# First product worked on in PSUM, softmax's small sums in one PSUM bank, every other weight chunk's low part on VectorE

## The chip, the cores and the metric

The kernel runs on one core of a Trainium2 chip. The metric is the device time of one execution in microseconds (us). Engines are named as the profile names them: PE is TensorE (matmuls, with PEld for its weight loads), DVE is VectorE, ACT is ScalarE, POOL is GpSimd, SP is SyncE, which issues the DMAs. All of them but SP work through instruction queues of their own, strictly in order.

## The reference, cut to what matters

Three stages follow each other: an attention with two kinds of masks, a two-layer MLP with a PReLU whose slope is given per hidden unit, and a routed mixture of eight experts.

```python
# attention: B, H, S, D = 4, 8, 576, 64
scores = scale * np.matmul(q, k.transpose(0, 1, 3, 2))
scores = np.where(masks[None, :, :, :], scores, -1000000000.0)   # local (heads 0-3) or strided (heads 4-7), both causal
scores = scores - np.max(scores, axis=-1, keepdims=True)
attn = np.exp(scores)
attn = attn / (np.sum(attn, axis=-1, keepdims=True) + 1e-09)
x = np.matmul(attn, v)                     # -> 2304 tokens x 512
# MLP, d_ff = 2048
h = x @ w_in
g = np.maximum(h, 0.0) + alpha * np.minimum(h, 0.0)
x = g @ w_out
# experts: the best of 8 by x @ w_gate, relu(x @ w1[e]) @ w2[e], weighted by the gate
```

## The kernel before, in words

**Attention.** The work is cut into groups (a pair of heads of one batch and some of its rows, four score blocks of up to 128 x 128 each, some groups two of 72 x 72). A step s of the attention lets each engine work on another group: ACT makes the exponentials of group s-1 (`att_exp`, L280, one ACTIVATE per block, each of which also sums its row into a column of `sm`), PE makes the scores of group s (`att_scores`, L228 and L234), PE and ACT make the values of group s-3 (`att_values`, `att_store`), PE transposes group s-2 (`att_transpose`, L312, copied out by ACT in L314), DVE takes the row maxima of group s (`att_max`: two reductions L252 and a scaling L255 of the small tile `nm`), and DVE and POOL normalize group s-1 (`att_norm`: L294 and L295 on the small tile `sm`, then L296 on POOL). Scores of a step lie in PSUM: in the first thirteen steps those of even steps in the first half of `sl_bank` and in bank X, those of odd steps in two banks "h"; in later steps always in `sl_bank` and X.

**Weights of the MLP.** They come in 16 chunks of float64 words. A chunk is decoded by ACT (`decode_a`, L401), DVE (`decode_b`, L405 and L406, and `decode_s`, L412) and then split into a high part by ACT (L420) and a low part by POOL (L421, 1024 columns of 128 partitions). The chunks 0 to 4 are decoded beside the first attention, the others one per iteration of the first block of the MLP.

**MLP.** Six blocks of 384 tokens, 16 chunks each; one chunk of one block is an iteration n. `mlp_in` makes the first product in one of the two banks "h" (12 matmuls, L438 to L440), `mlp_act` is the PReLU (ACT: L447 into the SBUF tile `a`, L448 into `bn`; DVE: L449 on both), `mlp_split` gives the high part `gh` (ACT, L458) and the low part `gl` (L460, on POOL in the first block, on DVE later), and `mlp_out` makes the second product (9 matmuls, L473 to L475). Iteration n issues the first product and the PReLU of n+2 and the second product of n, and in between up to one step of the attention.

**What sets the order.** The program's order is written by hand (`tc.manual_schedule()`), queue by queue. In the first block of the MLP, DVE's queue in iteration n reads: L294 and L295 of group s-1, L371 (the low part of the values of group s-3), L449 of n+2, the maxima of group s, then L405, L406 and L412 of chunk n+5. POOL's reads: L296, L421 of chunk n+4, L460 of n+2. The waits between the engines are put in by the program from what instructions write and read; in PSUM they go by whole banks.

Of the kernel before, what the change touches and what calls it, by code (L numbers as in the profile page):

```python
# [15 lines left out]
P = 128  # L16
# [11 lines left out]
BLK = 384  # L28
# [21 lines left out]
# Splits ahead of the turn of the tokens of the place after next, by the kinds of three places in a row.  # L50
# [3 lines left out]
# When the parts of the second plan, its lists and its indices come: (place, position).  # L54
WHEN = ((0, 7), (1, 1), (1, 1), (1, 4), (1, 6))
OHP = 12
# Groups that VectorE normalizes, and groups whose scores come after matmuls that keep TensorE awake.
NRV = (9,)
FS = {2: 2}
# Parts of the first two products of the MLP that run between the last steps of the first attention.  # L60
# [23 lines left out]
def attention_prelu_mlp_routed_experts_kernel(  # L84
# [40 lines left out]
    with tc.manual_schedule():  # L125
# [20 lines left out]
        # A visit is a pair of heads of a batch and the groups of its rows that are worked on in turn.  # L146
# [94 lines left out]

        def att_max(gi):
# [7 lines left out]
            if b < PE_MASK:  # L250
                for h2 in range(2):
                    nc.vector.tensor_reduce(  # L252
                        out=nm[:r, h2 * nj : (h2 + 1) * nj], in_=sc[h2][:r, 0:nj, :kk], axis=X, op=ALU.max, negate=True
                    )
                nc.vector.tensor_scalar_mul(nm[:r, :nu], nm[:r, :nu], SCALE)  # L255
# [15 lines left out]
        def att_exp(gi):  # L271
# [5 lines left out]
            sm = apool.tile([P, 4], F32, tag="sm", name="sm", bufs=3)  # L277
# [12 lines left out]
        def att_norm(gi):  # L290
            local, js, r, kk = shape_of(gi)
            nu = 2 * len(js)
            pt, sm = p_t[gi]
            nc.vector.tensor_scalar_add(sm[:r, :nu], sm[:r, :nu], 1e-9)  # L294
            nc.vector.reciprocal(sm[:r, :nu], sm[:r, :nu])  # L295
            (nc.vector if gi in NRV else nc.gpsimd).tensor_tensor(  # L296
                out=pt[:r, :nu, :kk],
                in0=pt[:r, :nu, :kk],
                in1=sm[:r, :nu].unsqueeze(2).to_broadcast([r, nu, kk]),
                op=ALU.mult,  # L300
            )
# [90 lines left out]
        # A weight comes as a float64, two words; it leaves as the sum of two float32r.  # L392
# [24 lines left out]
        def decode_c(c):  # L417
# [3 lines left out]
            nc.gpsimd.tensor_tensor(out=w[:, 1024:], in0=t, in1=w[:, :1024].bitcast(F32), op=ALU.subtract)  # L421
# [20 lines left out]
        def mlp_act(n):  # L442
            c = n % NC1
            ph = h_t.pop(n)
            a = xpool.tile([P, BLK], F32, tag="a", name="a", bufs=2)
            bn = xpool.tile([P, BLK], F32, tag="bn", name="bn", bufs=1)
            nc.scalar.activation(out=a, in_=ph[:, :BLK], func=AF.Relu)  # L447
            nc.scalar.activation(out=bn, in_=ph[:, :BLK], func=AF.Relu, scale=-1.0)  # L448
            nc.vector.scalar_tensor_tensor(  # L449
                out=a, in0=bn, scalar=nalpha[:, c : c + 1], in1=a, op0=ALU.mult, op1=ALU.add  # L450
            )
            h_t[n] = a

        def mlp_split(n):
            a = h_t.pop(n)
            gh = xpool.tile([P, BLK], F32R, tag="gh", name="gh", bufs=3)
            gl = xpool.tile([P, BLK], F32R, tag="gl", name="gl", bufs=2)
            nc.scalar.activation(out=gh, in_=a, func=AF.Copy)  # L458
            eng = nc.gpsimd if n < NC1 else nc.vector
            eng.tensor_tensor(out=gl, in0=a, in1=gh.bitcast(F32), op=ALU.subtract)  # L460
# [97 lines left out]
        def route_parts(blk):  # L558
            """One-hot choice, weight and place in its expert's list of each token of a block."""
# [76 lines left out]
        def plan_parts(early):  # L636
            """A column is a list of up to 128 tokens of one expert, a place's tokens one or two columns. The
            first EARLY columns hold pairs of full lists of the tokens before the last block. The others
            of each expert come in pairs from C_P on, a last odd one from C_S on; but a last one of FEW
            tokens or less has its column from C_Q on."""  # L640
# [209 lines left out]
        # A place is work on one expert: "P" on two columns, "S" on one, "Q" on one of few tokens. "P" makes  # L850
        # the hidden values with the tokens in the free dimension. "Q" takes the weights as they are, its
        # tokens stand in each quarter of the partitions, and each quarter makes its part of a row.
# [14 lines left out]
        def load_expert(t, h, always=False):  # L867
            """The first (h = 0) or second weight of place t's expert, unless it is there already."""
# [230 lines left out]
        def att_step(s, tags, ttag, vtag):  # L1099
            """One step of the attention, each engine's part on what the others did a step ago."""  # L1100
# [21 lines left out]
        def decode(k, n):  # L1122
            """The first n steps of a weight's decoding, those that are still to be done."""
# [40 lines left out]
        def gathers(ahead, places=NPL):  # L1164
            """The next tokens, as far as there is room for them."""
# [113 lines left out]
        def split(t, h, some=range(4)):  # L1279
            """Splits, and loads what comes next in the place of what was split."""  # L1280
# [103 lines left out]
        def some(kind, n, end, step):  # L1384
            """The places of a kind from the n-th on, as far as they are used, step by step."""
# [106 lines left out]
```

## Time and profile before

| | |
|---|---|
| median of three runs | 833.76 us (832.44 to 834.35) |
| span of the profiled execution, from the first to the last instruction | 831.9 us |
| median less that span, taken for what lies around it | 1.9 us |
| PE busy over the span | 784.2 us (94%) |
| DVE busy | 478.4 us (58%) |
| ACT busy | 427.3 us (51%) |
| POOL busy | 244.5 us (29%) |

The page's shares are means over stages with different limits. In the strip of 40 slices PE is at 9 tenths or more from the eighth slice (about 150 us) on nearly to the end, and between 6 and 8 tenths in the slices before, where DVE stands at 8 and 9 and POOL at 5 to 7. The stretch up to 150 us holds the first attention and the decoding of all 16 weight chunks.

### The profile page before, as it was taken

The numbers are of one execution on the slowest core, as the hardware profiler recorded it, in microseconds if no ns is written. First come the engines' busy times: TensorE is split into PE (matmuls) and PEld (weight loads), VectorE is DVE, ScalarE is ACT, GpSimd is POOL, SyncE is SP. The second block draws the span as 40 slices with busy tenths as digits, with TensorE's granted clock in tenths as the row PEclk, the third lists the DMA queues.
The fourth block names the chain that finished last, engine by engine and source line by source line (L and its number), as shares of the span: only waits on it lengthen the run. The fifth ranks groups of instructions, "written<-read, shape, count | busy, mean of one in ns | idle before, by whom it ended". The sixth has DMA issues, their size and how long they took to land. (4 is left out here: it accounts for less than half of the span.)

```text
span 831.9 us, 13663 instructions
## 1 busy us (share of the span) xinstructions
PE 784.2 (94%) x5032; PEld 659.6 (79%) x5035; DVE 478.4 (58%) x988; ACT 427.3 (51%) x1033; POOL 244.5 (29%) x168
## 2 busy tenths in 40 slices
PE   7687878999999999999999999999989998999995
PEld 4475766788888888888799898889878876878884
DVE  5989999345534554556333424757595447854422
ACT  6756665454455444665433333356534656655542
POOL 2756655200000000110000000032483354546422
PEclk9998999999999999999999999999999999999998
DMA  9716511101200121011000100362224577777421
GB/s 342 298 43 244 190 33 45 44 22 56 84 18 1 47 86 64 1 45 39 1 1 1 39 0 1 149 244 103 77 77 147 194 258 255 285 288 267 161 90 38
DMA packets 22621, 91.04 MB, mean 109 GB/s; under 512 B 3082, under 2 KB 7312, under 8 KB 15376
## 3 DMA queue, kind: packets, MB, share of 16 engines
q1 hardware_dynamic: 18816, 78.52, 26.6%
q0 software_dynamic: 3728, 11.55, 3.9%
q8 instruction: 41, 0.67, 0.3%
q14 instruction: 36, 0.29, 0.1%
HBM read 105.78 MB, written 9.97 MB: 139 GB/s over the span
## 5 line engine op out<-in xcount | busy, mean ns | idle before, releaser
L449 DVE SCALAR_TENSOR_TENSOR a<-bn,nalpha,a 128x384 f32<-128x384 f32 x96 | 73.2, 763 | 116.4 <-ACT bn L448 116.0
L438 PE MATMUL h<-xh,w 128*128 128x384 f32 x384 | 130.4, 340 | 0.4 <-ACT bn L448 0.4
L440 PE MATMUL h<-xh,w 128*128 128x384 f32 x384 | 129.9, 338 | 0.0
L439 PE MATMUL h<-xl,w 128*128 128x384 f32 x384 | 129.7, 338 | 0.0
L296 POOL TENSOR_TENSOR p<-p,sm 96x512 f32<-96x512 f32 (+2 forms) x47 | 48.7, 1036 | 267.6 <-DVE sm L295 255.3
L473 PE MATMUL acc<-w,gh 128*128 128x512 f32 x288 | 126.9, 441 | 0.0
L888 DVE TENSOR_TENSOR wx<-raw,wx 128x1024 fp32r<-128x1024 f32 x72 | 97.1, 1392 | 46.6 <-ACT wx L886 46.3
L475 PE MATMUL acc<-w,gl 128*128 128x512 f32 x288 | 115.8, 402 | 0.3 <-POOL gl L460 0.3
L474 PE MATMUL acc<-w,gh 128*128 128x512 f32 x288 | 115.6, 401 | 0.0
L886 ACT ACTIVATE wx<-raw 128x1024 fp32r<-128x1024 f32 x96 | 94.6, 1056 | 7.3 <-DMA raw<-in_wexp_dram 7.3
L447 ACT ACTIVATE a<-h 128x384 f32<-128x384 f32 x96 | 47.1, 491 | 99.7 <-PE h L440 99.6
L1042 PE MATMUL acc<-wx,hh 128*128 128x512 f32 x304 | 96.8, 400 | 0.0
L888 POOL TENSOR_TENSOR wx<-raw,wx 128x1024 fp32r<-128x1024 f32 x24 | 63.1, 2629 | 89.1 <-ACT wx L886 88.9
L438 PEld LDWEIGHTS h<-xh,w 128*128 128x128 f32 x384 | 73.1, 190 | 5.1 <-ACT bn L448 0.8
L439 PEld LDWEIGHTS h<-xl,w 128*128 128x128 f32 x384 | 72.9, 190 | 4.0
L440 PEld LDWEIGHTS h<-xh,w 128*128 128x128 f32 x384 | 72.6, 189 | 0.0
L895 POOL DMA_INDIRECT xg<-rows,idx_in x23 | 29.4, 1278 | 145.7 <-DVE a L449 139.3
L458 ACT ACTIVATE gh<-a 128x384 fp32r<-128x384 f32 x96 | 49.9, 520 | 42.6 <-DVE a L449 42.5
L475 PEld LDWEIGHTS acc<-w,gl 128*128 128x128 f32 x288 | 55.5, 193 | 14.2 <-POOL gl L460 0.8
L1042 PEld LDWEIGHTS acc<-wx,hh 128*128 128x128 f32 x304 | 56.5, 191 | 11.1
L473 PEld LDWEIGHTS acc<-w,gh 128*128 128x128 f32 x288 | 55.2, 192 | 11.1 <-issue 0.8
L460 DVE TENSOR_TENSOR gl<-a,gh 128x384 fp32r<-128x384 f32 x80 | 44.5, 556 | 28.7 <-ACT gh L458 16.6
(260 smaller groups left out, 1573.7 us busy)
## 6 DMA issues: line engine op xcount, KB each, us to landing
raw<-in_wexp_dram SPq DMA_DIRECT2D x64, 1024.0 KB
raw<-in_wp_dram SPq DMA_DIRECT2D x16, 1024.0 KB
qk<-in_qkv_dram SPq DMA_DIRECT2D x10, 576.0 KB
rows<-stage SPq DMA_DIRECT2D x15, 256.5 KB
v<-in_qkv_dram SPq DMA_DIRECT2D x8, 320.0 KB
qk<-in_qkv_dram SPq DMA_DIRECT2D x4, 384.0 KB
v<-in_qkv_dram SPq DMA_DIRECT2D x6, 256.0 KB
qk<-in_qkv_dram SPq DMA_DIRECT2D x4, 224.0 KB
```

Of the source, the lines that this page charges most:

```text
L296: (nc.vector if gi in NRV else nc.gpsimd).tensor_tensor(out=pt[:r, :nu, :kk], in0=pt[:r, :nu, :kk], in1=sm[:r, :nu].unsqueeze(2).to_broadc ...
L438: mm(ph[:, :BLK], w_in(c, 0, k), xh[:, k, :], start=(k == 0), stop=False)
L439: mm(ph[:, :BLK], w_in(c, 0, k), xl[:, k, :], start=False, stop=False)
L440: mm(ph[:, :BLK], w_in(c, 1, k), xh[:, k, :], start=False, stop=(k == KD - 1))
L449: nc.vector.scalar_tensor_tensor(out=a, in0=bn, scalar=nalpha[:, c : c + 1], in1=a, op0=ALU.mult, op1=ALU.add)
L458: nc.scalar.activation(out=gh, in_=a, func=AF.Copy)
L473: mm(o, gh[:, t], w_out(c, 0), start=(c == 0), stop=False)
L474: mm(o, gh[:, t], w_out(c, 1), start=False, stop=False)
L475: mm(o, gl[:, t], w_out(c, 0), start=False, stop=(c == NC1 - 1))
L886: nc.scalar.activation(out=w[:, :1024], in_=raw, func=AF.Copy)
L888: eng.tensor_tensor(out=w[:, 1024:], in0=raw, in1=w[:, :1024].bitcast(F32), op=ALU.subtract)
L1042: mm(po[i], h[:, h0 : h0 + P], wk[:, w0 : w0 + 512], start=st, stop=sp)
```

## The change

Three things are done. First, the PReLU works in the PSUM bank of the first product: ACT writes the second Relu back into the bank, DVE writes its result there, and both halves of the split read it there; the tile `bn` goes. The subtraction for `gl` is DVE's in every block. Second, two small tiles of the softmax get a stage in PSUM, in the last 64 columns of `sl_bank`: the row maxima before their scaling, and the sums of the exponentials; the scaled maxima and the sums with 1e-9 added still go to SBUF. Third, the low part of every odd weight chunk is subtracted by DVE instead of POOL.

```diff
+        def few(gi, n):
+            c = 448 + 32 * n + 4 * (gi % 8)
+            return sl_bank[:, c : c + 4]
...
             if b < PE_MASK:
+                raw = few(gi, 0)
                 for h2 in range(2):
                     nc.vector.tensor_reduce(
-                        out=nm[:r, h2 * nj : (h2 + 1) * nj], in_=sc[h2][:r, 0:nj, :kk], axis=X, op=ALU.max, negate=True
+                        out=raw[:r, h2 * nj : (h2 + 1) * nj], in_=sc[h2][:r, 0:nj, :kk], axis=X, op=ALU.max, negate=True
                     )
-                nc.vector.tensor_scalar_mul(nm[:r, :nu], nm[:r, :nu], SCALE)
+                nc.vector.tensor_scalar_mul(nm[:r, :nu], raw[:r, :nu], SCALE)
...
-            sm = apool.tile([P, 4], F32, tag="sm", name="sm", bufs=3)
+            sm = few(gi, 1)
...
-            pt, sm = p_t[gi]
-            nc.vector.tensor_scalar_add(sm[:r, :nu], sm[:r, :nu], 1e-9)
+            pt, raw = p_t[gi]
+            sm = apool.tile([P, 4], F32, tag="sm", name="sm", bufs=3)
+            nc.vector.tensor_scalar_add(sm[:r, :nu], raw[:r, :nu], 1e-9)
...
-            nc.gpsimd.tensor_tensor(out=w[:, 1024:], in0=t, in1=w[:, :1024].bitcast(F32), op=ALU.subtract)
+            eng = nc.vector if c % 2 else nc.gpsimd
+            eng.tensor_tensor(out=w[:, 1024:], in0=t, in1=w[:, :1024].bitcast(F32), op=ALU.subtract)
...
+            v = ph[:, :BLK]
             a = xpool.tile([P, BLK], F32, tag="a", name="a", bufs=2)
-            bn = xpool.tile([P, BLK], F32, tag="bn", name="bn", bufs=1)
-            nc.scalar.activation(out=a, in_=ph[:, :BLK], func=AF.Relu)
-            nc.scalar.activation(out=bn, in_=ph[:, :BLK], func=AF.Relu, scale=-1.0)
+            nc.scalar.activation(out=a, in_=v, func=AF.Relu)
+            nc.scalar.activation(out=v, in_=v, func=AF.Relu, scale=-1.0)
             nc.vector.scalar_tensor_tensor(
-                out=a, in0=bn, scalar=nalpha[:, c : c + 1], in1=a, op0=ALU.mult, op1=ALU.add
+                out=v, in0=v, scalar=nalpha[:, c : c + 1], in1=a, op0=ALU.mult, op1=ALU.add
             )
-            h_t[n] = a
+            h_t[n] = v
...
-            nc.scalar.activation(out=gh, in_=a, func=AF.Copy)
-            eng = nc.gpsimd if n < NC1 else nc.vector
-            eng.tensor_tensor(out=gl, in0=a, in1=gh.bitcast(F32), op=ALU.subtract)
+            nc.scalar.activation(out=gh, in_=v, func=AF.Copy)
+            nc.vector.tensor_tensor(out=gl, in0=v, in1=gh.bitcast(F32), op=ALU.subtract)
```

Since PSUM is tracked by whole banks, the small sums bring waits with them. DVE's queue at the start of the attention (steps 0 and 1; in brackets whose count an instruction waits for) reads before:

```order
L252 TENSOR_REDUCE nm<-sl_bank 96x2 [waits PE_49]
L252 TENSOR_REDUCE nm<-X 96x2 [waits PE_49]
L255 TENSOR_SCALAR nm<-nm 96x4 [waits DVE_49]
L252 TENSOR_REDUCE nm<-h 96x2 [waits PE_49] x2
L255 TENSOR_SCALAR nm<-nm 96x4 [waits DVE_49]
L294 TENSOR_SCALAR sm<-sm 96x4 [waits Activation_49]
```

and now (lines stand seven further on in the changed kernel):

```order
L258 TENSOR_REDUCE sl_bank<-sl_bank 96x2 [waits PE_49]
L258 TENSOR_REDUCE sl_bank<-X 96x2 [waits DVE_49,PE_49]
L261 TENSOR_SCALAR nm<-sl_bank 96x4 [waits DVE_49]
L258 TENSOR_REDUCE sl_bank<-h 96x2 [waits DVE_49,PE_49,Activation_49]
L258 TENSOR_REDUCE sl_bank<-h 96x2 [waits DVE_49,PE_49]
L261 TENSOR_SCALAR nm<-sl_bank 96x4 [waits DVE_49]
L301 TENSOR_SCALAR sm<-sl_bank 96x4
```

The second reduction of a group now waits for the first, and the reductions of step 1 wait for ACT: for the last exponential of step 0, which writes its sum into the same bank.

ACT's exponentials of steps 0 and 1 stand like this before:

```order
L280 ACTIVATE p,sm<-sl_bank,nm 96x128 [waits DVE_49,PE_49]
L280 ACTIVATE p,sm<-sl_bank,nm 96x128
L280 ACTIVATE p,sm<-X,nm 96x128 [waits PE_49]
L280 ACTIVATE p,sm<-X,nm 96x128
L280 ACTIVATE p,sm<-h,nm 96x128 [waits DVE_49,PE_49]
```

and now:

```order
L286 ACTIVATE p,sl_bank<-sl_bank,nm 96x128 [waits DVE_49,PE_49]
L286 ACTIVATE p,sl_bank<-sl_bank,nm 96x128 [waits Activation_49]
L286 ACTIVATE p,sl_bank<-X,nm 96x128 [waits PE_49,Activation_49]
L286 ACTIVATE p,sl_bank<-X,nm 96x128 [waits Activation_49]
L286 ACTIVATE p,sl_bank<-h,nm 96x128 [waits DVE_49,PE_49,Activation_49]
```

Each exponential now waits for ACT's own one before it. The matmuls of an even step's scores, which write `sl_bank`, wait in the same way for the last exponential of the step before (their rows read alike in both programs; the count that they wait for is another).

In the first block of the MLP, one iteration of DVE's queue reads before, from the maxima of a group to the PReLU of the next iteration:

```order
L252 TENSOR_REDUCE nm<-sl_bank 126x2 [waits PE_49]
L252 TENSOR_REDUCE nm<-X 126x2 [waits PE_49]
L255 TENSOR_SCALAR nm<-nm 126x4 [waits DVE_49]
L405 TENSOR_SCALAR stage<-stage 128x1024
L406 SCALAR_TENSOR_TENSOR stage<-raw_581,stage 128x1024 [waits DMAHW3_49,DVE_49]
L412 SCALAR_TENSOR_TENSOR stage<-raw_581,stage 128x1024 [waits DVE_49]
L294 TENSOR_SCALAR sm<-sm 126x4 [waits Activation_49]
L295 RECIPROCAL sm<-sm 126x4 [waits DVE_49]
L371 TENSOR_TENSOR xl<-T,xh 128x192 [waits Activation_49]
L449 SCALAR_TENSOR_TENSOR a<-bn,nalpha,a 128x384 [waits Activation_49,Pool_49]
```

and now, from the same step of the program, with the PReLU ahead of it:

```order
L457 SCALAR_TENSOR_TENSOR h<-h,nalpha,a 128x384 [waits Activation_49]
L429 TENSOR_TENSOR w<-stage,w 128x1024 [waits Activation_49]
L258 TENSOR_REDUCE sl_bank<-sl_bank 126x2 [waits PE_49]
L258 TENSOR_REDUCE sl_bank<-X 126x2 [waits DVE_49,PE_49]
L261 TENSOR_SCALAR nm<-sl_bank 126x4 [waits DVE_49]
L412 TENSOR_SCALAR stage<-stage 128x1024
L413 SCALAR_TENSOR_TENSOR stage<-raw_581,stage 128x1024 [waits DMAHW3_49,DVE_49]
L419 SCALAR_TENSOR_TENSOR stage<-raw_581,stage 128x1024 [waits DVE_49]
L467 TENSOR_TENSOR gl<-h,gh 128x384 [waits PE_49,Activation_49]
L301 TENSOR_SCALAR sm<-sl_bank 126x4 [waits Activation_49]
```

L429, the low part of an odd chunk, has come in between the PReLU and the maxima, and L467, the low part of the hidden values, between the decoding and the normalization. The wait of the PReLU for POOL is gone, and its bank "h" is free for PE only when L467 has read it.

## Rows read from the trace of the kernel before

**Rows 1.** Windows: stretch, length, busy PE, PEld, DVE, ACT, POOL, PE clock, DMA share, GB/s.

```profile
15.00:50.16 35.16, 25.26 (x188) 16.99 (x187) 34.38 (x68) 24.89 (x84) 22.86 (x11) 0.90 0.61 245
60.73:141.18 80.45, 64.55 (x373) 50.47 (x372) 78.88 (x106) 51.94 (x144) 47.31 (x29) 0.91 0.37 137
200.00:300.00 100.00, 99.96 (x631) 84.56 (x630) 49.35 (x144) 49.28 (x161) 9.10 (x10) 1.00 0.12 41
```

**Rows 2.** Timeline, 99.5 to 101 us, DVE and POOL: start, duration, instruction, idle before.

```profile
99.60 0.47 DVE L371 TENSOR_TENSOR xl<-T,xh 128x84 fp32r<-128x84 f32 x2
99.82 1.04 POOL L296 TENSOR_TENSOR p<-p,sm 96x512 f32<-96x512 f32 x1 [2.77 <-DVE sm L295]
99.98 3.67 DVE L449 SCALAR_TENSOR_TENSOR a<-bn,nalpha,a 128x384 f32<-128x384 f32 x1
...
100.82 2.42 POOL L421 TENSOR_TENSOR w<-stage,w 128x1024 fp32r<-128x1024 f32 x1
```

**Rows 3.** Groups by line, DVE, 60.73 to 141.18 us: count, busy, mean ns, idle.

```profile
L406 DVE SCALAR_TENSOR_TENSOR stage<-raw,stage 128x1024 int32<-128x1024 int32 x10 | 18.5, 1848 | 0.3
L449 DVE SCALAR_TENSOR_TENSOR a<-bn,nalpha,a 128x384 f32<-128x384 f32 x11 | 18.3, 1665 | 0.2 <-issue 0.2
L255 DVE TENSOR_SCALAR nm<-nm 96x4 f32<-96x4 f32 (+2 forms) x10 | 16.9, 1692 | 0.3
```

**Rows 4.** Timeline of DVE, 137 to 163 us, where POOL runs nothing beside the row.

```profile
137.57 0.68 DVE L405 TENSOR_SCALAR stage<-stage 128x1024 int32<-128x1024 int32 x1
...
139.54 1.22 DVE L412 SCALAR_TENSOR_TENSOR stage<-raw,stage 128x1024 int32<-128x1024 int32 x1
...
161.10 0.62 DVE L449 SCALAR_TENSOR_TENSOR a<-bn,nalpha,a 128x384 f32<-128x384 f32 x1 [4.04 <-ACT bn L448]
162.31 0.56 DVE L460 TENSOR_TENSOR gl<-a,gh 128x384 fp32r<-128x384 f32 x1 [0.59 <-ACT gh L458]
```

**Rows 5.** Timeline, 7 to 20 us, steps 0 to 4 of the attention.

```profile
7.11 0.41 DVE L252 TENSOR_REDUCE nm<-X 96x2 f32<-96x256 f32 x1
7.55 0.17 DVE L255 TENSOR_SCALAR nm<-nm 96x4 f32<-96x4 f32 x1
...
14.49 0.27 PE L228 MATMUL X<-cst 126*126 126x252 bf16 x1 [0.37 <-ACT p L280]
...
14.91 0.37 ACT L280 ACTIVATE p<-h,nm 96x128 f32<-96x128 f32 x1
...
15.16 0.21 ACT L280 ACTIVATION_READ_ACCUMULATOR p<-h,nm 96x1 f32 x1
15.25 0.37 ACT L280 ACTIVATE p<-h,nm 96x128 f32<-96x128 f32 x1
...
16.64 0.55 PE L312 MATMUL T<-cst,p 96*128 96x96 f32 x4
...
17.28 0.49 ACT L314 ACTIVATE ptt<-T 128x384 f32<-128x384 f32 x1 [0.50 <-PE T L312]
...
18.39 1.15 ACT L401 ACTIVATE stage<-raw 128x1024 f32<-128x1024 f32 x1 [0.47 <-DMA raw<-in_wp_dram]
...
19.43 0.37 ACT L280 ACTIVATE p<-sl_bank,nm 126x126 f32<-126x126 f32 x1
```

**Rows 6.** Groups by line, DVE, 20.3 to 50.16 us: steps 5 to 12.

```profile
L412 DVE SCALAR_TENSOR_TENSOR stage<-raw,stage 128x1024 int32<-128x1024 int32 x5 | 8.8, 1766 | 0.0
L406 DVE SCALAR_TENSOR_TENSOR stage<-raw,stage 128x1024 int32<-128x1024 int32 x4 | 6.3, 1578 | 0.1
L255 DVE TENSOR_SCALAR nm<-nm 126x4 f32<-126x4 f32 (+1 forms) x5 | 4.1, 819 | 0.2
...
L294 DVE TENSOR_SCALAR sm<-sm 126x4 f32<-126x4 f32 (+1 forms) x6 | 3.1, 520 | 0.0
```

**Rows 7.** Timeline, 211 to 215 us, the second block of the MLP.

```profile
212.83 0.17 DVE L294 TENSOR_SCALAR sm<-sm 96x4 f32<-96x4 f32 x1 [0.92 <-ACT p L280]
...
213.09 0.35 PE L234 MATMUL sl_bank<-qk 64*96 64x128 f32 x1
```

More of the change, by code (lines that the diff above doesn't have):

```diff
@@ L444, in mlp_act @@
             ph = h_t.pop(n)
+            v = ph[:, :BLK]
             a = xpool.tile([P, BLK], F32, tag="a", name="a", bufs=2)
-            bn = xpool.tile([P, BLK], F32, tag="bn", name="bn", bufs=1)
-            nc.scalar.activation(out=a, in_=ph[:, :BLK], func=AF.Relu)
-            nc.scalar.activation(out=bn, in_=ph[:, :BLK], func=AF.Relu, scale=-1.0)
+            nc.scalar.activation(out=a, in_=v, func=AF.Relu)
+            nc.scalar.activation(out=v, in_=v, func=AF.Relu, scale=-1.0)
             nc.vector.scalar_tensor_tensor(
-                out=a, in0=bn, scalar=nalpha[:, c : c + 1], in1=a, op0=ALU.mult, op1=ALU.add
+                out=v, in0=v, scalar=nalpha[:, c : c + 1], in1=a, op0=ALU.mult, op1=ALU.add
             )
-            h_t[n] = a
+            h_t[n] = v
         def mlp_split(n):
-            a = h_t.pop(n)
+            v = h_t.pop(n)
             gh = xpool.tile([P, BLK], F32R, tag="gh", name="gh", bufs=3)
             gl = xpool.tile([P, BLK], F32R, tag="gl", name="gl", bufs=2)
-            nc.scalar.activation(out=gh, in_=a, func=AF.Copy)
-            eng = nc.gpsimd if n < NC1 else nc.vector
-            eng.tensor_tensor(out=gl, in0=a, in1=gh.bitcast(F32), op=ALU.subtract)
+            nc.scalar.activation(out=gh, in_=v, func=AF.Copy)
+            nc.vector.tensor_tensor(out=gl, in0=v, in1=gh.bitcast(F32), op=ALU.subtract)
             g_t[n] = (gh, gl)
```

## The prediction, made before the changed kernel was run

> **What bounds the kernel now.** I read the strip of slices first, then the windows. From about 150 us on PE is the limit: in a stretch of the second block it is busy 99.96 of 100 us [rows 1]. There a cheaper DVE or POOL instruction gives nothing, and a new wait can only cost. Before that DVE is the limit: 78.88 of 80.45 us busy in ten iterations of the first block, while PE idles 15.9 us of them at a granted clock of 0.91, and 34.38 of 35.16 us in the attention ahead of it [rows 1]. So the change is decided before 150 us, in two stages: the attention up to the first PReLU (L449, 50.16 us) and the iterations after it, which take 80.45 / 10 = 8.05 us each.
>
> Why DVE is so busy is read from single rows. L449 works on two SBUF tiles and takes 0.62 us when POOL is idle [rows 4], but 3.67 us when it is issued at 99.98: POOL's L296 has just begun (99.82), L421 follows it to 103.24, and DVE is through 0.4 us later [rows 2]. L371, which reads one tile from PSUM and one from SBUF, ran through at 0.47 us for two beside the same L296 [rows 2]. So DVE stands still while POOL runs, for instructions with two SBUF inputs; and for the tiny scaling L255, which reads and writes SBUF, as well: mean 1.69 us in the iterations against 0.17 us free [rows 3, 5]. An instruction of POOL that follows another at once keeps DVE out through both.
>
> The Trainium skill ("SBUF — State Buffer", Who interferes with whom) states this as a rule: DVE with two SBUF inputs or in a two-port mode and POOL exclude each other for a whole instruction, DVE with one SBUF input doesn't. The rows agree, and by that rule alone the change could only gain.
>
> **What leaves and what comes on DVE.** In an iteration L255 and L449 cease to stand in POOL's way, since their inputs come from PSUM: together they lose (1.69 - 0.17) + (1.67 - 0.62) = 2.6 us [rows 3 to 5]. POOL loses L460 in every iteration and L421 (2.4 us) in every other. DVE gains L460 in every iteration (0.5 us from start to next start, by 0.56 us [rows 4]) and the low part of every odd chunk. No row has that on DVE; it is the kind of L460 with 1024 in place of 384 columns, so between 1.0 us (the slope of L406, 1.22 us for 1024 columns with more to do, less a little) and 0.56 x 1024 / 384 = 1.5 us; I take 1.2. PSUM as an output has no row; L371's 0.24 us with a PSUM input says that reading costs nothing visible; I take the PReLU in PSUM at 0.6 us, and 0.5 to 0.9 us as bounds.
>
> **What the shared bank adds.** The sums lie in `sl_bank`, and waits go by bank. Three follow. (a) The second reduction of a group starts after the first has ended, as L255 does now: 7.52 ended, 7.55 started [rows 5]. A group's maxima take 1.05 us where they took 0.95. (b) Four exponentials of a group stand 0.34 us apart, since the next begins beside the reading of the sum (14.91, 15.25; the sum is there at 15.37) [rows 5]. Now the next waits for that reading: 0.46 us and 0.02 for the wait, 0.48 apart. A group takes 1.9 us until its last sum is there, not 1.5. (c) Steps run after each other: the maxima of step s wait for the exponentials of s-1, the exponentials of s for DVE's addition to the sums of s-1, and an even step's scores for the exponentials of s-1.
>
> The Trainium skill ("PSUM — Partial Sum Buffer", PSUM bank collisions raise a hardware error) says that two engines may not use one bank on the same partitions at once, not even in different columns. It speaks against the change: by it these waits can't be left out. Were they, the first stage below would not lose its 10.3 us, and the sum would be 826.
>
> **First stage, to the PReLU of chunk 0.** In step 4 the scores begin on X at 14.49, end at 15.39, and step 3's exponentials run beside them from 14.91 [rows 5]. Walked by the new waits from the first maxima (6.76): exponentials of step 0 end at 9.8; maxima and addition, exponentials of step 1, 11.0 to 12.9; scores of step 2, 13.9; transposes and copy 15.2, decoding by ACT 16.2; exponentials of step 2 to 18.2; maxima 19.2; exponentials of step 3, 19.4 to 21.3; scores of step 4 to 22.3, then, as in the rows, 1.8 us to the end of the transposes (15.39 to 17.19), 0.5 for the copy and 1.1 for L401, which stand ahead on ACT [rows 5]. The exponentials of step 4 start at 25.8 and not at 19.43, and the maxima of step 5 at 27.7, not 20.3.
>
> From there DVE sets the pace again. Before, it needs 29.9 us to 50.16. Of these 8.8 - 5 x 1.22, 6.3 - 4 x 1.22, 4.1 - 5 x 0.17 and 3.1 - 6 x 0.16 = 9.5 us are standstill beside POOL [rows 6], so 20.4 us are work. Now two low parts of chunks (1, 3) come to it, 2.4 us, and some 1.0 us of waits for itself. What it stands still I walk: the low part of chunk 0 and the normalization ahead of it keep L405 out for 3.2 us, those of chunk 2 for 3.3, normalizations alone 1.7, and it waits for ACT 1.2 us: 9 us, as before, because the blocked instruction is only another. 27.7 + 20.4 + 3.4 + 9 = 60.5. **Loss 10.3 us.** Bounds: if POOL blocked nothing, the chain of exponentials alone would still end at about 57 (loss 6.8); with each blocked turn falling badly, 62.5 (loss 12.3).
>
> **Second stage, iterations.** From the end of one L412: L460 0.5, addition 0.2 (0.7), reciprocal, L371, L449 (1.8), scores are ready at 0.7 + 1.2 = 1.9, maxima to 2.95. POOL starts the normalization at 1.0 and ends it at 2.05. Even chunk: its low part follows, 2.05 to 4.45; L405 is kept out from 2.95 on; L405 to L412 take 3.1 (137.57 to 140.7 [rows 4]); 7.55. Odd chunk: DVE's low part is kept out to 2.05, ends at 3.25, maxima 4.3, then 3.1: 7.4. In two of nine iterations the normalization is short (72 columns), 0.6 us less. Mean 7.35, against 8.05: nine iterations, -6.3. The two iterations ahead of them: the PReLU of chunk 2 now waits for a bank that L460 of chunk 0 frees, +0.5, and the first with an odd chunk -0.9. At the end the last decoding leaves L449 standing 3.2 us less, of which the lengthened exponentials and PE, which then is late, keep half: -1.5. **Gain 8.2 us.** Bounds: an iteration can't be shorter than ACT's and PE's own round (scores 1.0, second product and transposes 1.1, copy 0.4, L401 1.1, gh 0.5, exponentials 1.9, addition and scores' start 0.4: 6.4 us), nor do I see it above 8.0.
>
> **After 150 us.** New waits fall on the limiting PE: scores wait for the addition to the sums. In 23 steps the scores began 0.1 to 1.7 us after it (0.09 in [rows 7]: 213.00 to 213.09); exponentials that take 0.4 us more eat this up in three places: +0.6 us, at most 1.8. The bank "h" is held until L460 has read it, 1.7 us or more ahead of need in all iterations but one: 0.3 at most. The experts are not touched.
>
> **Sum.** 831.9 + 10.3 - 8.2 + 0.6 = 834.6 us span; with the 1.9 us by which the median stands above the profiled span, **836.5 us**. Two large terms of opposite sign decide; within their likely errors the forecast covers 832 to 839.
>
> **Rivals.** *Relief wins (faster).* Place: the iterations. If POOL's remaining low parts fall beside the maxima and the PReLU, which now run from PSUM, an iteration gets near 6.4 to 6.7 us: 9 x 1.45 + 2 = 15 us gained, and the first stage, by the same cause, loses 7 to 8. -7 + 0.6: 827 (825 to 830). It decides below 7.05 us an iteration, where nine give 9 and the gain passes the loss. For it: more than a third of DVE's time in the iterations is standstill [rows 3]; against it: the even chunk's low part can't begin before 2.05 and DVE has only 0.9 us of PSUM work left by then.
> *ACT gets late (slower still).* Longer exponentials push the two Relus and L420, so that the low parts start a microsecond later in each iteration: 8.0 us, gain only 3 us: 842. Against it: ACT is busy 51.94 of 80.45 us [rows 1].
> *It doesn't do what it says:* PSUM inputs are kept out as well; L371 speaks against it. Then DVE has only more work, and it is 845 or more.
>
> **Chances.** Forecast 0.45, relief 0.33, ACT late 0.20, last 0.02. A difference under 0.2% (1.7 us) can't be told from none. Of the forecast 0.18 falls within it (832.1 to 835.4), 0.02 below, 0.25 above. Faster 0.35, same 0.18, slower 0.47. Range 825 to 844: it takes in relief's middle and ACT's lateness.
>
> **What would show it.** First stage: the exponentials 0.48 us apart, those of step 4 near 25.8, the first PReLU at 57 to 62. Iterations: L449's and L255's successors near 0.6 and 0.17 us each, the standstill moved to L405, about 7.35 us from PReLU to PReLU. After 150 us PE as full as before. If exponentials stay 0.34 apart or step 4's start stays near 20, the shared bank costs nothing and relief wins; if L405 isn't kept out, too.

## The result: slower by 1.5%

| | before | changed |
|---|---|---|
| median of the runs side by side (four each) | 834.06 us (832.44 to 835.48) | 847.77 us (844.32 to 848.90) |
| ratio | | 1.0148, 95% interval 1.0109 to 1.0187 |
| span of the profiled execution | 831.9 us | 842.4 us |
| PE / DVE / ACT / POOL busy | 784.2 / 478.4 / 427.3 / 244.5 us | 785.8 / 465.8 / 432.0 / 198.9 us |

The forecast was 836.5 us with a range of 825 to 844. The direction was its likelier one, the size was not: 13.7 us were lost where 2.7 were forecast, and the time lies above the range. The profiled execution was the shortest of the four, so the traces show 10.5 us of the 13.7; two later traces (last experiment) show where longer executions differ.

### The profile page after: what moved, and what is told of

Same layout as the page of the kernel before. It is cut to its first block, busy times and chain, and to the rows that moved or that the text cites. A ratio compares the mean times of both kernels' runs of the same rounds, so it can differ in the third digit from the quotient of the medians.

```text
span 842.4 us, 13708 instructions
## 1 busy us (share of the span) xinstructions
PE 785.8 (93%) x5035; PEld 663.1 (79%) x5035; DVE 465.8 (55%) x1012; ACT 432.0 (51%) x1033; POOL 198.9 (24%) x144
## 5 line engine op out<-in xcount | busy, mean ns | idle before, releaser
L446 PE MATMUL h<-xh,w 128*128 128x384 f32 x384 | 130.7, 340 | 2.4 <-DVE gl L467 2.4
L457 DVE SCALAR_TENSOR_TENSOR h<-h,nalpha,a 128x384 f32<-128x384 f32 x96 | 60.0, 625 | 117.4 <-ACT h L456 117.3
L303 POOL TENSOR_TENSOR p<-p,sm 96x512 f32<-96x512 f32 (+2 forms) x47 | 45.8, 975 | 325.0 <-DVE sm L302 274.6
L446 PEld LDWEIGHTS h<-xh,w 128*128 128x128 f32 x384 | 73.1, 190 | 7.2 <-DVE gl L467 3.1
L467 DVE TENSOR_TENSOR gl<-h,gh 128x384 fp32r<-128x384 f32 x96 | 53.3, 555 | 31.5 <-PE acc L482 17.8
L466 ACT ACTIVATE gh<-h 128x384 fp32r<-128x384 f32 x96 | 46.8, 487 | 33.3 <-DVE h L457 33.2
```

Source lines behind the costliest of these rows:

```text
L446: mm(ph[:, :BLK], w_in(c, 0, k), xh[:, k, :], start=(k == 0), stop=False)
L457: nc.vector.scalar_tensor_tensor(out=v, in0=v, scalar=nalpha[:, c : c + 1], in1=a, op0=ALU.mult, op1=ALU.add)
L467: nc.vector.tensor_tensor(out=gl, in0=v, in1=gh.bitcast(F32), op=ALU.subtract)
```

## The profile after

The windows of the changed kernel that answer to [rows 1]: the attention up to the first PReLU, ten iterations of the first block, and 100 us of the second block. (Lines stand six to eight further on in the changed kernel: the PReLU is L457, the exponentials L286, the maxima L258 and L261, the addition to the sums L301, the low part `gl` L467, the low part of a chunk L429, the decoding L412, L413 and L419.)

```profile
core 0: us, PE busy (x) PEld busy (x) DVE busy (x) ACT busy (x) POOL busy (x), PEclk, DMA share, GB/s
15.00:62.60 47.60, 31.23 (x211) 20.16 (x209) 34.81 (x75) 29.94 (x95) 15.77 (x10) 0.82 0.46 177
75.83:152.13 76.30, 61.48 (x371) 50.45 (x369) 69.07 (x121) 52.36 (x144) 19.97 (x14) 0.93 0.40 146
210.00:310.00 100.00, 99.84 (x631) 84.30 (x630) 49.20 (x143) 50.15 (x159) 9.10 (x10) 1.00 0.12 40
```

The second block is as full on PE as before. The ten iterations are 4 us shorter (76.30 against 80.45), with POOL relieved of more than half its work. The first stage is what is long: the first PReLU starts at 62.60 us and not at 50.16, and DVE, which was busy 34.38 of 35.16 us there, is busy 34.81 of 47.60. It does no more work; it waits. The waits of DVE from the first maxima of step 5 (28.86 us) to the first PReLU:

```profile
engine line waited for: us in total, times, longest us
DVE sl_bank L258 <- ACT p L286: 3.3, 3, 1.4
DVE w L429 <- ACT w L427: 1.8, 2, 1.1
DVE xl L378 <- ACT xh L373: 1.1, 1, 1.1
```

The first row is the shared bank: the maxima of a step (written to `sl_bank`) wait for the exponentials of the step before (whose sums go to the same bank). How such a step runs is read in the timeline of steps 0 to 3 (start, duration, engine, line; in brackets the idle time before and who ended it):

```profile
7.89 0.36 ACT L286 ACTIVATE p<-X,nm 96x128 f32<-96x128 f32 x1
8.34 0.36 ACT L286 ACTIVATE p<-X,nm 96x128 f32<-96x128 f32 x1
8.79 0.96 DVE L258 TENSOR_REDUCE sl_bank<-h 96x2 f32<-96x256 f32 x2 [1.91 <-ACT p L286]
9.87 0.15 DVE L301 TENSOR_SCALAR sm<-sl_bank 96x4 f32<-96x4 f32 x1
10.13 0.36 ACT L286 ACTIVATE p<-h,nm 96x128 f32<-96x128 f32 x1 [1.37 <-DVE sm L301]
...
11.96 0.37 PE L228 MATMUL sl_bank<-cst 96*96 96x256 bf16 x1 [4.78 <-ACT p L286]
...
19.43 0.36 ACT L286 ACTIVATE p<-h,nm 96x128 f32<-96x128 f32 x1 [0.21 <-DVE sm L301]
```

Exponentials stand 0.45 us apart (7.89, 8.34) and not 0.34 [rows 5]. DVE stands 1.91 us until they are through, ACT stands 1.37 us until DVE has added to the sums, PE stands 4.78 us until the odd step's exponentials are through. Engines that worked beside one another now take turns.

A table of the PReLU's starts, read from the trace of each kernel that ran, divides the time by stages. A column is the start of the first PReLU, the time from it to that of chunk 2, from chunk 3 to chunk 12 (nine iterations; in brackets one), from chunk 12 to 16, and the span.

| kernel | first PReLU | to chunk 2 | 3 to 12 | 12 to 16 | span |
|---|---|---|---|---|---|
| before | 50.16 | 4.08 | 71.63 (7.96) | 28.74 | 831.9 |
| changed | 62.60 | 7.01 | 68.97 (7.66) | 26.08 | 842.4 |
| sums and maxima alone | 64.61 | 4.09 | 71.68 (7.96) | 28.12 | 848.5 |
| PReLU alone | 50.16 | 6.99 | 67.79 (7.53) | 25.13 | 827.6 |
| odd chunks alone | 52.18 | 4.11 | 69.23 (7.69) | 28.72 | 834.2 |
| PReLU and odd chunks | 51.94 | 7.00 | 64.75 (7.19) | 24.82 | 825.9 |
| changed, sums in SBUF | 52.74 | 7.01 | 66.88 (7.43) | 24.81 | 830.6 |
| changed, maxima in SBUF | 60.56 | 7.01 | 66.57 (7.40) | 27.73 | 840.8 |
| changed, PE kept at work | 59.89 | 6.53 | 68.87 (7.65) | 27.64 | 842.9 |
| PReLU from chunk 2, odd chunks | 52.06 | 4.93 | 63.87 (7.10) | 24.82 | 827.0 |
| the same, spread maxima | 51.76 | 4.24 | 64.79 (7.20) | 24.81 | 825.7 |
| PReLU from chunk 2, all chunks | 51.52 | 4.83 | 61.85 (6.87) | 24.38 | 824.0 |

By it the changed kernel loses 12.44 us up to the first PReLU and 2.93 to chunk 2, gains 0.3 to chunk 3, 2.66 in the nine iterations and 2.66 behind them, and loses 0.7 in all that follows: 10.5. Two of these numbers hold scatter. The first maxima begin at 6.76 us in the kernel before and at 5.72 in the changed one (5.72 to 6.77 over all kernels), so from the first maxima on the first stage loses 13.5 us and not 12.4. And the 0.7 us are 0.3 lost up to chunk 90, 0.9 gained from there to the last PReLU, and 1.3 lost behind it, in a stage that the change doesn't touch and that took between 274.3 us (before) and 279.8 us (the fastest kernel of the table).

## The experiments

**One part at a time.** The four kernels are the parts of the change. The first has `few` and its uses alone:

```diff
+                raw = few(gi, 0)
...
+            sm = few(gi, 1)
```

> The kernel before with the small sums and maxima in the score bank alone; PReLU and low parts as before. Theory 'bank': the waits of the shared bank make the first stage long, so this part alone carries the loss: exponentials 0.46 us apart, exponentials of step 3 at about 19.4 us, TensorE's granted clock under 0.8 in 12 to 18 us, first PReLU at 60 to 62 us (50.16 before), iterations still near 8 us since the PReLU stands still beside GpSimd; the time 8 to 14 us above before (842 to 848). Rival 'work': the loss comes from the work that VectorE takes over (low parts of chunks and of the split), which this kernel doesn't have; then the first PReLU is at 50 to 53 us and the time within 3 us of before.

Measured: 850.33 us, ratio 1.0181 (1.0153 to 1.0209). The first PReLU is at 64.61 us, beyond the 60 to 62 expected; an iteration takes 7.96 us as before. By the medians this part alone costs more than the whole change (15.4 against 13.7 us), and 'work' falls.

The second has the PReLU and its split alone:

```diff
-            nc.scalar.activation(out=bn, in_=ph[:, :BLK], func=AF.Relu, scale=-1.0)
+            nc.scalar.activation(out=v, in_=v, func=AF.Relu, scale=-1.0)
...
-            eng = nc.gpsimd if n < NC1 else nc.vector
-            eng.tensor_tensor(out=gl, in0=a, in1=gh.bitcast(F32), op=ALU.subtract)
+            nc.vector.tensor_tensor(out=gl, in0=v, in1=gh.bitcast(F32), op=ALU.subtract)
```

> The kernel before with the PReLU worked on in PSUM and the split's subtraction on VectorE, nothing else. 'Bank' (of the scores): first PReLU near 50 us as before; the chunk 2 PReLU 1 to 3 us later after the first than before (the first product of chunk 2 waits until the low part of chunk 0 is read from its bank), then iterations shorter by 0.4 to 0.8 us each, so 828 to 833 us. 'Work': VectorE gains 0.5 us an iteration and the standstill moves to the decoding, so nothing is won and the time is 834 to 840.

Measured: 829.42 us, ratio 0.9928 (0.9901 to 0.9954). The first PReLU is at 50.16 us to the hundredth, that of chunk 2 loses 2.9 us, an iteration gains 0.43.

The third has the odd chunks alone:

```diff
-            nc.gpsimd.tensor_tensor(out=w[:, 1024:], in0=t, in1=w[:, :1024].bitcast(F32), op=ALU.subtract)
+            eng = nc.vector if c % 2 else nc.gpsimd
+            eng.tensor_tensor(out=w[:, 1024:], in0=t, in1=w[:, :1024].bitcast(F32), op=ALU.subtract)
```

> The kernel before with the low part of every odd weight chunk on VectorE, nothing else. 'Bank': small either way: the first PReLU at 49 to 52 us, odd iterations shorter and even ones as before, 829 to 836 us. 'Work': two more VectorE instructions of 1.2 us stand in the limiting queue of the first stage and in every other iteration: first PReLU 2 us or more late, 836 to 842.

Measured: 834.28 us, ratio 0.9986 (0.9968 to 1.0003): no difference. Two low parts more cost the first stage 2.0 us, as 'work' said, and the iterations give them back.

The fourth has both of these, and SBUF for the small tiles (shown against the changed kernel; the maxima go back likewise):

```diff
-            sm = few(gi, 1)
+            sm = apool.tile([P, 4], F32, tag="sm", name="sm", bufs=3)
...
```

> The changed kernel with the small sums and maxima back in SBUF (PReLU in PSUM and odd chunks on VectorE stay). 'Bank': first PReLU back at 50 to 52 us, clock 1.00 in 12 to 18 us, iterations of 7.3 to 7.9 us; the time 12 to 20 us under the changed kernel, 826 to 835. 'Work': still 840 or more, with the first PReLU at 55 us or later.

Measured: 828.20 us, ratio 0.9913 (0.9884 to 0.9941). So the change holds a gain of 6.7 us (834.89 - 828.20) and a loss of 19.6 us (847.77 - 828.20). By the medians the loss is larger than the 15.4 us of the small tiles alone; by the profiled executions it is the same, 16.5 us (842.4 - 825.9) against 16.6 (848.5 - 831.9), but the table shows it in other places. Alone, the small tiles cost 14.5 us up to the first PReLU and leave an iteration at 7.96 us. On top of the other parts they cost 10.7 us up to the first PReLU and lengthen an iteration from 7.19 to 7.66. A reading of this, which no run isolates, is that in the iterations their waits lay beside DVE's standstill and come to light when that is gone.

**Sums or maxima.** Of the changed kernel one of the two small tiles goes back to SBUF. Sums in SBUF, maxima in PSUM:

```diff
-            sm = few(gi, 1)
+            sm = apool.tile([P, 4], F32, tag="sm", name="sm", bufs=3)
...
```

> The changed kernel with the sums of the exponentials back in SBUF; only the raw row maxima stay in the score bank. Theory 'sums': it is the write of each exponential's sum into the bank that binds the steps to one another (exponential to exponential, scores of an even step to the exponentials before it, exponentials to the addition). Then nearly all of the loss goes: exponentials 0.34 us apart again, first PReLU at 52 to 56 us (62.6 in the changed kernel, 51.9 with both small tiles in SBUF), 828 to 835 us. Rival 'maxima': the reductions of a step, which wait for exponentials that read the bank, carry it; then the first PReLU stays at 58 us or later and the time at 840 or more.

Measured: 832.54 us, ratio 0.9971 (0.9955 to 0.9987), first PReLU at 52.74, exponentials 0.34 us apart.

Maxima in SBUF, sums in PSUM:

```diff
-                raw = few(gi, 0)
...
-                        out=raw[:r, h2 * nj : (h2 + 1) * nj], in_=sc[h2][:r, 0:nj, :kk], axis=X, op=ALU.max, negate=True
+                        out=nm[:r, h2 * nj : (h2 + 1) * nj], in_=sc[h2][:r, 0:nj, :kk], axis=X, op=ALU.max, negate=True
...
```

> The changed kernel with the raw maxima back in SBUF; only the sums stay in the score bank. 'Sums': first PReLU at 59 to 63 us, exponentials 0.46 us apart, 842 to 848 us. 'Maxima': first PReLU at 52 to 56 us, 828 to 836 us.

Measured: 844.36 us, ratio 1.0117 (1.0097 to 1.0138), first PReLU at 60.56, exponentials 0.45 us apart. The sums carry the loss of the first stage: of the 10.7 us between 51.94 and 62.60 they make 8.6 alone, the maxima 0.8 alone; the rest needs both. In the iterations each of the two costs about 0.2 us (7.40 and 7.43 against 7.19), and neither pays for itself.

**The clock.** In the changed kernel the granted clock falls where PE waits. Windows of the kernel before, then of the changed one:

```profile
12.00:18.00 6.00, 5.47 (x58) 3.39 (x56) 4.38 (x10) 5.37 (x23) 2.28 (x2) 1.00 1.03 421
18.00:24.00 6.00, 3.87 (x37) 2.35 (x37) 5.83 (x17) 4.75 (x16) 4.36 (x3) 1.00 1.01 399
```

```profile
12.00:18.00 6.00, 6.00 (x36) 3.58 (x36) 1.26 (x5) 3.03 (x10) 1.04 (x1) 0.52 1.03 422
18.00:24.00 6.00, 3.43 (x21) 1.92 (x21) 4.86 (x10) 2.56 (x11) 1.60 (x1) 0.77 0.91 355
```

The column behind POOL is the granted clock: 0.52 after PE's 4.78 us of waiting, nearly all of it at the lower level, 1.2 GHz, where it was 1.00 before. PE's busy time is fuller with fewer matmuls, because each takes longer. The scores of step 2 take 1.7 us (11.96 to 13.65) where 0.9 were taken [rows 5], and they lie on the chain. The experiment gives PE dummy matmuls while it waits:

```diff
-FS = {2: 2}
+FS = {2: 12, 4: 8, 6: 8, 8: 8}
```

> The changed kernel with dummy matmuls on zeros ahead of the scores of steps 2, 4, 6 and 8 (12 and 8 each; before only step 2 has two). Theory 'clock': TensorE's granted clock fell to 0.52 in 12 to 18 us because TensorE stood waiting there, and the scores of each even step took 1.7 us where 0.9 was taken before; kept at work, its clock stays at 0.9 or more, scores take about 0.9 us, the first PReLU comes 2 to 3.5 us earlier (59 to 60.6 us) and the time is 2 to 3.5 us under the changed kernel (844 to 846). Rival 'waits alone': the clock is no part of the loss; the first PReLU stays at 62 to 64 us and the time at 847 to 850.

The dummies of step 2, and windows:

```profile
7.63 2.76 PE L216 MATMUL acc<-zeros 128*128 128x512 bf16 x12
```

```profile
12.00:18.00 6.00, 4.98 (x35) 3.17 (x34) 1.25 (x5) 3.26 (x13) 1.50 (x2) 0.72 1.02 423
18.00:24.00 6.00, 4.66 (x36) 2.53 (x35) 4.87 (x10) 3.02 (x14) 1.60 (x1) 1.00 0.96 377
24.00:30.00 6.00, 4.45 (x36) 2.62 (x37) 4.13 (x16) 5.45 (x17) 1.37 (x2) 1.00 0.64 238
30.00:36.00 6.00, 5.03 (x45) 2.87 (x43) 5.19 (x9) 3.83 (x14) 6.00 (x3) 1.00 0.32 72
```

Measured: 844.46 us (843.92 to 845.69), ratio to before 1.0113 (1.0093 to 1.0134). That median is 3.3 us under the changed kernel's, but the intervals of the two ratios overlap, and the profiled executions are equally long (842.9 and 842.4 us): what this one gained at the start it lost between chunk 12 and 16 and behind the last PReLU. The first stage is what the traces tell apart. In step 2 the clock still fell (0.72 in 12 to 18 us, scores from 13.02 to 14.37). From 18 us on it stays at 1.00, step 4's scores start at 21.96 and its exponentials at 26.26: 4.3 us, against 5.8 in the changed kernel (21.26 to 27.03). The first PReLU comes at 59.89, although the first maxima started at 6.77 in this execution and not at 5.72. From the first maxima to the first PReLU it is 53.1 us, where the three traces of the changed kernel (two more stand in the last experiment) have 56.9, 57.4 and 59.3. So more work for PE makes the first stage shorter, and at least 2.7 us of its 12.4 are the clock.

**The held bank.** The PReLU of chunk 2 loses 2.9 us in every kernel that works in PSUM from chunk 0 on. The first product of chunk 2 in the changed kernel (L446) and what stands ahead of it:

```profile
62.60 0.63 DVE L457 SCALAR_TENSOR_TENSOR h<-h,nalpha,a 128x384 f32<-128x384 f32 x1 [0.40 <-ACT h L456]
63.26 0.49 ACT L466 ACTIVATE gh<-h 128x384 fp32r<-128x384 f32 x1 [0.69 <-DVE h L457]
63.78 0.56 DVE L467 TENSOR_TENSOR gl<-h,gh 128x384 fp32r<-128x384 f32 x1 [0.56 <-ACT gh L466]
64.39 0.69 PE L446 MATMUL h<-xh,w 128*128 128x384 f32 x1 [2.22 <-DVE gl L467]
64.88 0.52 PE L447 MATMUL h<-xl,w 128*128 128x384 f32 x1
```

Before, the second Relu of chunk 0 released it, a microsecond ahead of the first PReLU:

```profile
49.13 0.44 PE L438 MATMUL h<-xh,w 128*128 128x384 f32 x1 [0.44 <-ACT bn L448]
```

Now it is released by the low part `gl`, 1.8 us behind that PReLU, and after a wait of 2.2 us its matmuls take 0.52 us where 0.33 is the time at the full clock. The experiment does chunks 0 and 1 as before and works in PSUM from chunk 2 on, with the small tiles in SBUF and the odd chunks on DVE:

```diff
+            bn, res = v, v
+            if n < 2:
+                bn, res = xpool.tile([P, BLK], F32, tag="bn", name="bn", bufs=1), a
...
```

> The changed kernel with both small tiles in SBUF, and with the PReLU of chunks 0 and 1 as before (second Relu into SBUF, result in SBUF, low part by GpSimd); from chunk 2 on it works in PSUM. Theory 'held bank': the 2.9 us that the chunk 2 PReLU loses against the first come from the first product of chunk 2, which waits until the low part of chunk 0 is read from the bank. They go, so the PReLU of chunk 2 comes 2.1 us after that of chunk 1, as before, and the time is 1.5 to 3 us under that of the kernel with PReLU in PSUM and odd chunks (824.5 to 827 by 828.2). Rival 'work': the lag is VectorE's own work or the clock; then it stays, and the time is 827 to 829.

Measured: 825.72 us (824.65 to 829.05), ratio 0.9883 (0.9864 to 0.9902), 2.5 us under the kernel that works in PSUM from the start (828.20), though the intervals of the two ratios overlap. From the first PReLU to that of chunk 2 it takes 4.93 us: 2.1 of the 2.9 are gone. The rest stayed: the product now begins at 52.08, right after the second Relu, but still runs at the lower clock:

```profile
52.08 0.58 PE L439 MATMUL h<-xh,w 128*128 128x384 f32 x1 [0.42 <-ACT bn L452]
52.45 0.53 PE L440 MATMUL h<-xl,w 128*128 128x384 f32 x1
```

In the trace of the next experiment, whose chunks 0 and 1 are done in the same way, these matmuls are back at 0.34 us half-way through the product, and the stretch takes 4.24 us, 0.2 more than before.

**Can the scaling of the maxima escape POOL in SBUF?** The kernel of the last experiment, with the maxima in every other column of a wider tile:

```diff
-            nm = apool.tile([P, 4], F32, tag="nm", name="nm", bufs=2)
+            nm = apool.tile([P, 8], F32, tag="nm", name="nm", bufs=2)[:, ::2]
```

> As the kernel with PReLU in PSUM from chunk 2 on and odd chunks on VectorE, small tiles in SBUF; the scaled maxima are written to every other column of their tile. Theory 'port form': the tiny scaling of the maxima stands still beside GpSimd because it reads and writes packed columns; spread out it runs through at about 0.17 us (mean 0.73 in the iterations of the kernel with PReLU and odd chunks), the standstill moves on to the decoding, and iterations are 0 to 0.4 us shorter: 822 to 826 us. Rival 'any SBUF to SBUF': it still stands still for a microsecond or more beside GpSimd and the time doesn't change (824.5 to 827).

Measured: 827.84 us (825.14 to 828.34), ratio 0.9893 (0.9865 to 0.9921); no gain. The row of L255 in the nine iterations, without the spread and with it:

```profile
L255 DVE TENSOR_SCALAR nm<-nm 126x4 f32<-126x4 f32 (+2 forms) x9 | 5.6, 617 | 0.3
```

```profile
L255 DVE TENSOR_SCALAR nm<-nm 126x4 f32<-126x4 f32 (+2 forms) x9 | 5.6, 619 | 0.3
```

'Port form' falls: packed or spread, from SBUF to SBUF it stands still beside POOL.

**All low parts on DVE.**

```diff
-            eng = nc.vector if c % 2 else nc.gpsimd
+            eng = nc.vector
```

> As the kernel with PReLU in PSUM from chunk 2 on, small tiles in SBUF, but VectorE makes the low part of every weight chunk, GpSimd of none. Theory 'standstill': an even chunk's low part on GpSimd takes 2.4 us during which the decoding on VectorE stands still, on VectorE it takes 1.2 us; iterations with even chunks come to the 7.0 us or so of those with odd ones, and in the first stage three more of them do the same: 819 to 825 us. Rival 'load': VectorE is the busiest engine and gets 1.2 us more work where GpSimd's share was partly covered by PSUM work; 825 to 831 us.

Measured: 824.97 us (821.89 to 825.88), ratio 0.9855 (0.9826 to 0.9884): 1.5% faster than before, the lowest median of all. Between 'standstill' (819 to 825) and 'load' (825 to 831) the time alone doesn't decide, and its interval overlaps that of the kernel without this step (0.9864 to 0.9902); the iterations do. The nine of them, as a window and by groups of DVE's instructions (busy us, mean ns, idle before):

```profile
62.05:123.90 61.85, 55.79 (x346) 43.86 (x344) 60.48 (x112) 46.61 (x129) 7.18 (x9) 0.97 0.47 173
```

```profile
L422 DVE TENSOR_TENSOR w<-stage,w 128x1024 fp32r<-128x1024 f32 x9 | 13.7, 1518 | 0.1
L406 DVE SCALAR_TENSOR_TENSOR stage<-raw,stage 128x1024 int32<-128x1024 int32 x9 | 11.0, 1225 | 0.3
L255 DVE TENSOR_SCALAR nm<-nm 126x4 f32<-126x4 f32 (+2 forms) x9 | 1.5, 168 | 0.3
```

DVE is the limit (60.48 of 61.85 us) and yet an iteration takes 6.87 us, the least of all, although DVE has one more instruction of 1.2 us in every second one: L255 and L406 run through at 0.168 and 1.225 us, and only L422 still stands still, 0.3 us each, beside L296. In the nine iterations DVE was busy 62.50 us with the even chunks on POOL and is busy 60.48 without: POOL's 2.4 us for a low part had cost DVE more than making it costs.

**Where the other 3 us are.** The changed kernel twice more, for its trace.

> The changed kernel once more, unchanged, for a second trace: the profiled execution was the shortest of its four (span 842.4 us, the others 845.2 to 847.0). Theory 'end': a longer execution differs behind the last PReLU of the MLP, in the experts' stage (275.6 us from there to the end in the first trace), by 2 to 5 us, with the first PReLU at 62.6 us again. Rival 'first stage': the first PReLU itself comes 2 us or more later, since the clock there falls at other moments.

> The changed kernel a third time, for the same question and with the same two answers: the length behind the last PReLU of the MLP (275.6 us in the first trace), or the start of the first PReLU (62.6 us).

Measured: spans of 848.4 and 849.0 us. Both answers hold a part. All maxima up to step 7 start within 0.06 us of the first trace; then the third trace differs in 42 to 50 us (the first trace ahead, the third below):

```profile
42.00:50.00 8.00, 5.02 (x48) 2.98 (x47) 6.95 (x18) 5.61 (x22) 1.02 (x1) 1.00 0.25 85
```

```profile
42.00:50.00 8.00, 6.30 (x39) 3.70 (x39) 5.56 (x11) 3.74 (x14) 1.03 (x1) 0.59 0.02 7
```

PE comes to the scores of step 8 after the same wait of 3.32 us in both traces; a matmul of theirs then takes 0.27 us in the first and 0.42 in the third. At a granted clock of 0.59 there the third trace comes 2.4 us later to the first PReLU (65.02). The second trace has 0.69 there, is 0.55 us late at the first PReLU and 2.1 us late at the last. Behind the last PReLU both take 279.5 and 279.8 us and not 275.6; but the kernel before took 838.14 us beside them, and the kernels with the PReLU in PSUM from chunk 2 on, though faster, took 277.9 to 279.8 there, so that part need not be the change's. Why the clock falls in one execution and not in the next is open.

## Why the prediction was wrong

- **What bounds the kernel: right.** All but 0.7 us of the losses and gains lie before 171 us, and the second block is as full on PE as it was.
- **DVE's single costs: right.** L457 took 0.62 us (0.6 forecast), L261 0.16, L467 0.55, the low part of a chunk 1.23 (1.2). The standstill moved to the decoding as forecast: L412 took 1.50 us in the mean of ten iterations where its free time is 0.68.
- **The shared bank's waits: right in kind.** Exponentials 0.45 us apart (0.48 forecast), a group's maxima 1.16 us (1.05 forecast), step 3's exponentials at 19.43 (19.4). The kernels with sums and with maxima apart say which of the two small tiles weighs: the sums.
- **First stage: the step that failed is the walk's durations.** It took PE's times from rows at the full clock and did not ask what the new waits do to the clock. The loss is 12.44 us, 10.3 were forecast, with 12.3 as the upper bound; with PE kept at work it is 9.73. Piece by piece: from the first maxima to those of step 5 the walk has 20.9 us (6.76 to 27.7), the changed kernel 23.1 (5.72 to 28.86), the kernel with PE kept at work 21.3 (6.77 to 28.08); from there to the first PReLU 32.8, 33.7 and 31.8. That the changed execution began 1.0 us earlier than the walk assumed was luck, and hides as much of the miss. The trace of before had the sign: in the stages where PE idles [rows 1] shows 0.90 and 0.91. The reason given for the walk's second half was wrong too, though its length was near: DVE does not set the pace again from step 5 on, it stands idle 6.35 of the 33.74 us to the first PReLU, 3.3 of them for exponentials:

```profile
28.86:62.60 33.74, 20.86 (x136) 14.07 (x136) 27.39 (x56) 20.84 (x63) 12.10 (x7) 0.84 0.31 115
```

- **Chunk 2: mis-sized.** 0.5 us was put for the first product that waits for L467; it cost 2.9, 2.1 by the wait and the rest by matmuls at the lower clock. The prediction names this wait and gives no working for its 0.5 us; in the two first iterations product, PReLU and split follow each other with nothing in between.
- **Iterations: the term that was half wrong.** 7.35 us were forecast, 7.66 measured, 7.96 before. (The forecast took 8.05 for before, a mean over ten iterations; of the 3.6 us that its nine iterations are off, 0.8 are this base and 2.8 the length.) Without the small tiles the same work gives 7.19, so DVE's and POOL's part of the walk was right, even cautious. What failed is that it followed these two engines alone: it let the scores wait for the addition and found this hidden beside DVE's work, and did not follow what PE's standstill does to the rest of PE's queue. In nine iterations PE waits 12.3 us for the additions; without the small tiles it stands idle 8.7 us there in all. DVE stands idle 7.0 us (busy 61.98 of 68.97) against 2.15 (62.60 of 64.75) without the small tiles; the trace names the end of 4.4 us of it, 2.0 of them ACT's copy of the values, which itself waits for PE. Of the changed kernel PE's wait in the nine iterations, the window of them and, in one of them, the addition that the scores wait for; then the nine iterations of the kernel without the small tiles:

```profile
PE sl_bank L228 <- DVE sm L301: 12.3, 7, 4.2
```

```profile
75.83:144.80 68.97, 56.69 (x344) 46.52 (x343) 61.98 (x109) 47.31 (x129) 17.57 (x13) 0.93 0.41 154
```

```profile
104.57 0.15 DVE L301 TENSOR_SCALAR sm<-sl_bank 72x2 f32<-72x2 f32 x1
104.76 0.27 PE L228 MATMUL sl_bank<-cst 96*96 96x256 bf16 x1 [1.46 <-DVE sm L301]
```

```profile
65.18:129.93 64.75, 56.03 (x347) 44.15 (x345) 62.60 (x108) 46.61 (x129) 17.66 (x13) 0.97 0.45 166
```

- **After 150 us: right as far as the walk went.** 0.3 us were lost between chunk 16 and chunk 90, 0.6 forecast. That the whole of it comes to 0.7 is luck: the 0.9 us gained up to the last PReLU and the 1.3 lost behind it were not in the sum.
- **The rivals.** *Relief* had the right mechanism for the PReLU and the chunks; but its place was a kernel without the small sums, which takes 828.20. *ACT gets late* gave 842 by iterations longer than forecast; they were, at 7.66 us, but not by ACT's work, which is 47.31 us in the nine iterations and 46.61 without the small tiles: ACT waits for PE, 17.7 us against 10.5. *It doesn't do what it says* has the nearest number, 845 or more, by a cause that did not occur: with PSUM inputs L457 ran through at 0.62 us.
- **The page on bank collisions.** The Trainium skill ("PSUM — Partial Sum Buffer", PSUM bank collisions raise a hardware error) was weighed as speaking against the change. The program has the waits that it asks for, and the trace shows them at work: exponentials, maxima, scores and additions came one after another. No run here shows what would happen without the waits.
- **Sum.** Forecast: 10.3 + 0.5 - 0.9 - 6.3 - 1.5 + 0.6 = 2.7. Traced: 12.4 + 2.9 - 0.3 - 2.7 - 2.7 + 0.7 = 10.3, by rounding 0.2 under the spans' 10.5. The three steps above make 2.1 + 2.4 + 3.6 of the 7.8 us between, the rest is small terms of both signs. The other 3.4 us or so of the miss in the median lie between the changed kernel's profiled execution and its median, 5.4 us where the forecast added 1.9. The range was too narrow above: its upper end was ACT's lateness with the first stage at its middle, and the two bad ends together were left out although one cause, the waits of the shared bank, moves both.

## What to carry to other kernels

Before a small tile goes to PSUM, ask not only which instruction it speeds up but who else uses its bank: the sums of the exponentials in the bank of the scores made PE, ACT and DVE take turns and cost some 16 us (844.36 us with the sums there, 828.20 with both small tiles in SBUF). No run gave the sums a bank of their own, so what they would cost there is open. When a chain gets new waits on TensorE, cost its matmuls again at the lower clock, and look at the first iterations apart from the steady ones. Where VectorE stands still beside GpSimd, count what an instruction on GpSimd costs both of them: 2.4 us on GpSimd were dearer than 1.2 us more on VectorE, the busiest engine.

## What the runs showed of the hardware

- 34 more dummy matmuls in PE's waits brought the first PReLU 2.7 us forward: the granted clock stayed at 1.00 from 18 us to 42 us (0.62 to 0.95 in the changed kernel, by windows of 6 us), and the chain's own matmuls with it.
- The clock's fall differs between executions of one kernel at the same work: 1.00, 0.69 and 0.59 in 42 to 50 us, with all maxima up to step 7 equal within 0.06 us; the first PReLU starts 0.55 and 2.4 us later in the two slower ones.
- A scaling of four columns from SBUF to SBUF takes up to 2.38 us beside POOL (0.17 without it), with a spread tile as with a packed one; from PSUM it took 0.16 us in every iteration. The Trainium skill ("SBUF — State Buffer", Who interferes with whom) counts `tensor_scalar`, which this is, among the instructions that can enter a two-port mode and then exclude GpSimd; both rows agree.
